# Attention and a Fourier-mixing block on one Trainium2 core: token fold with repeated operands, whole 128x128 transposes, and a new order of the work

## The chip, the cores and the metric

The kernel runs on one core of a Trainium2 chip. The engines of the core work side by side: PE multiplies matrices, DVE, ACT and POOL work on vectors, and SP here only issues DMA transfers, as ACT and POOL also do. Every engine runs its own list of instructions strictly in order and waits at an instruction whose inputs are not there. The metric is the time of one execution in microseconds (us); the number that counts is the median of several runs.

## The reference, cut to what matters

```python
def reference(q, k, v, w1, w2):            # q, k, v: 4 batches, 8 heads, 768 tokens, 64
    s = q @ k.T / 8 - slope[h] * dist      # keys kept: the first 8, and the last 96 before the query
    x = softmax(where(keep, s, -1e9)) @ v  # -> x: 4 x 768 x 512
    u = x + real(fft(fft(x, axis=tokens), axis=features))
    un = (u - mean(u)) / sqrt(var(u) + 1e-6)
    return u + relu(un @ w1) @ w2          # w1: 512 x 2048, w2: 2048 x 512
```

## The kernel before, in words

**Three layers of work.** PE's work falls into units, and every unit carries a name. `A0` to `A76` are attention units: scores of a band of keys (`sc`, L729, L737, L743), or `pav`, the product with v (L822). `M0` to `M32` are mixing units, which do the two Fourier transforms as matrix products: `pf` (L1013) folds the tokens of batch 0 and `px` (L1165) spreads them, `py` (L1105) is the product along one axis, `pu` (L1192) the one along the other; its result with x added is `u`. The transposes of the normalised `un` into `unT` are M units too (`ptu`, L1309). `H0` to `H95` are blocks of the first product of the feed-forward part (`ph`, L1339: 8 matmuls of 128 x 256), and `G0` to `G66` are parts of the second.

**Pair-chunks.** Each batch's tokens are cut into 3 pair-chunks of 256 tokens, 12 in all, numbered c=0 to 11, each with 8 `ph` blocks. Chunks 0 and 1 do the second product plainly (`pg`, L1370, 64 matmuls of 128 x 512 together). From chunk 2 on it is done with seven products in place of eight (`pgA` and `pgD`, L1484, evacuated by DVE at L1502). These need four sums per chunk of halves of the hidden layer, `s1` to `s4`, each one 128 x 1024 addition in 16 bits (`eg`, `sb`, `hT`). `s2`, `s3` and `s4` wait for earlier sums of their chunk, and `s1` for the chunk's hidden blocks.

**Transposing un.** For c=0 to 2 PE does it, with 64 x 64 transposes into one PSUM tile `ptu`, copied out at L1321. For c=3 to 11 the DMA does it from SP's queue (L1292).

**Fold.** The token fold (two units on PE, each for two heads' columns) forms six sums of x's token blocks, with the identity, minus the identity and plus or minus half of it as weights: 32 matmuls of 128 columns into one `pf` tile.

**x by way of DRAM.** For batch 1 and later, x is written to DRAM when it is finished (`xd`: L872 and L874, from ACT's queue) and read back twice in the order in which `u` needs it: `xr` in rows by SP's queue (L884), and mirrored rows by an indirect DMA of POOL (L887), which needs the small table `back`. DVE adds them when it evacuates `pu` (L1232 and L1244). `distk` is another table, from which ACT and DVE make the masks `mk` of batches 2 and 3.

**w1 and w2** come as eight DMAs of 512 KB from POOL's queue (L1674). Part j of w1 holds hidden blocks 2j and 2j+1.

**What sets the order.** A class `Plan` holds a table `ORDER`, one list of names for each engine: unit names for PE, and for the others names such as `H5.0` (an evacuation or a follow-up of unit H5) and `T.91` (a DMA, a table, a sum). `Plan.run` issues the work in that order; its costs and due times place instructions that are not free in the list, but on each engine the list decides. Evacuations can be on ACT (`hT`, L1344) or DVE (L1345), as the list says. Where a list names `T.91`, the xr read-back of batch 1, as next on SP, everything behind it in SP's list stands until its inputs are there.

Of the kernel before, what the change touches and what calls it, by code (L numbers as in the profile page):

```python
# [24 lines left out]
class Plan:  # L25
# [9 lines left out]
    MIX = 1.3  # L35
    LANDED = {"HW": 0.55, "SW": 1.3}
    LAT = {"ACT": 0.14, "DVE": 0.12, "POOL": 0.08}
# [84 lines left out]
    def op_go(self, eng, name, start):  # L122
# [6 lines left out]
        if eng == "POOL":  # L129
            self.ports.append((start, end, 1 if dma else 0 if outs and outs[0][0] in ("vB", "kB") else 2))  # L130
        if dma:
            at = max(max(end + 0.55, 5.5) if eng == "POOL" else end + lat + 2.7 * (lat == 1.0 and end > 3.5), self.now)
# [19 lines left out]

    SHARED = {"kB": 1, "vB": 1, "sid": 1, "f1": 0, "f2": 0, "f3": 0, "z": 0, "g0": 0, "w": 0, "s": 0, "w2a": 0, "w2t": 0, "ex": 0}
# [3 lines left out]
    def beside(self, start, cost, kind):  # L157
# [4 lines left out]
        if names:  # L162
            s = self.op_start("POOL", names[-1])
            if s is not None:
                p = self.made[names[-1]]
                ports = ports + [(max(s, start), max(s, start) + p[0]["POOL"][0], 1 if p[7] else 0 if p[3] and p[3][0][0] in ("vB", "kB") else 2)]
# [15 lines left out]
    def move(self, go=False):  # L182
# [38 lines left out]
    def unit_start(self, unit):  # L221
# [7 lines left out]
        if not there:  # L229
# [114 lines left out]
def act(n):  # L344
    return 0.1 + n / 1180.0
# [10 lines left out]
def pool(n):  # L356
    return 0.16 + n / 1080.0


@with_exitstack  # L360
def kernel(
# [156 lines left out]
    def load_v(b, hp):  # L518
        h0 = 2 * hp
        if b >= FB:  # L520
# [3 lines left out]
            swq(whole, 1.08, [("avdone", b - 2), ("wl", 7)], [("v", b, hp, t) for t in range(2)], (1536, 0.93), False)  # L524
            return
        if b == 1:
            for t in range(2 - hp % 2 * 2):
# [3 lines left out]
                swq(four, 1.08, [], [("v", b, hp, t), ("v", b, hp + 1, t)], (1536, 0.93))  # L531
            return
        for t in range(2):
# [3 lines left out]
            swq(run, 0.85, ([("avdone", b - 2), ("wl", 7)] if b > 1 else []), [("v", b, hp, t)], (768, 0.93), b < 2)  # L537
# [4 lines left out]
    def load_qk(b, hp):  # L542
# [3 lines left out]
        for w, src in enumerate((q, k)):  # L546
            if b >= FB:
                for h in range(2):
# [4 lines left out]
                    swq(run, 0.85, free(tag, ti) + [("wl", 7)], [("qk", n, w, h)], (768, 0.93), False)  # L553
# [25 lines left out]
            if n == 4:  # L579
# [5 lines left out]
                swq(two, 1.08, free(tag, ti), [("qk", n, w), ("qk", n + 1, w)], (1536, 1.53))  # L585
# [7 lines left out]
            swq(run, 0.85, free(tag, ti), [("qk", n, w)], (768, 1.53))  # L593
# [110 lines left out]
    def score(b, hp, g):  # L704
# [3 lines left out]
        def run(start, ring):  # L708
# [37 lines left out]
            e = pl.pe((0.45, 0.45, 0.34)[g] if pem else 0.24, start, "64x64" if pem else "64x32")  # L746
# [203 lines left out]
    def fold_0():  # L950
# [53 lines left out]
        def fold_pe(hp):  # L1004
            cols = slice(hp * P, (hp + 1) * P)

            def run(start, ring):
                zy()
                pf = bank(ring, f"pf_{hp}")
                for n, terms in enumerate(ZS):  # L1010
                    o = pf[:, n // 4, (n % 4) * P:(n % 4 + 1) * P]
                    for x, (w, i) in enumerate(terms):
                        nc.tensor.matmul(o, w, X[0][:, i, cols], start=(x == 0), stop=(x == len(terms) - 1))  # L1013
# [775 lines left out]
```

## Time and profile before

| | |
|---|---|
| runs | 247.54, 247.75, 249.1 us; median 247.75 us |
| profiled execution | 245.87 us, with a span of 244.1 us; granted TensorE clock 0.991 |
| PE busy | 232.0 us (95% of the span) |
| DVE busy | 193.4 us (79%) |
| ACT busy | 138.8 us (57%) |
| POOL busy | 114.8 us (47%) |
| DMA moved | 32.85 MB |

The span is from the first to the last instruction of the profiled execution; 1.8 us of its own time lie outside the span. The median of the other runs is 1.9 us above the profiled one. Busy PE counts a matmul from its start to a modelled end, and matmuls overlap their neighbours, so starts are more exact than busy times: a unit's cost is read from the start of its first matmul to the start of the next unit.

### The profile page before, as it was taken

What the parts mean: (1) busy time and instruction counts of PE and PEld (TensorE: products, weight loads), DVE (VectorE), ACT (ScalarE), POOL (GpSimd) and SP (SyncE); (2) the same over time, 40 slices, a digit from 0 to 9 for tenths busy, and PEclk for the clock granted to TensorE, in tenths of its full rate; (3) what the DMA queues carried; (4) which work ended last, traced back from release to release, by engine and by line L of the source; (5) the groups of instructions that cost most, each with busy time, mean ns of one, the idle gap of its engine ahead of it and who ended that gap; (6) DMA issues with size and microseconds to landing.
All of it is one profiled execution on the core that took longest, in us unless ns stands there. A gap on an engine that the chain in (4) does not pass through costs nothing.

```text
span 244.1 us, 7606 instructions
## 1 busy us (share of the span) xinstructions
PE 232.0 (95%) x3251; PEld 191.2 (78%) x3251; DVE 193.4 (79%) x420; ACT 138.8 (57%) x226; POOL 114.8 (47%) x164
## 2 busy tenths in 40 slices
PE   7679899999999999999999999999999999999993
PEld 2557776878677667788989888898889898888883
DVE  2559997879972789999999889889998755846483
ACT  2368788864657468658357788364534651434200
POOL 8998898866590038999059056500300320011020
PEclk9997999999999999999999999999999999999999
DMA  6999999999999999999999979220570330040212
GB/s 170 181 169 145 157 235 172 197 190 196 110 145 152 234 179 205 117 135 110 242 184 285 135 84 156 46 33 13 174 258 4 77 99 0 1 130 1 89 72 99
DMA packets 95938, 32.85 MB, mean 135 GB/s; under 512 B 84160, under 2 KB 92480, under 8 KB 95904
## 3 DMA queue, kind: packets, MB, share of 16 engines
q0 software_dynamic: 66176, 17.06, 71.7%
q1 hardware_dynamic: 26560, 12.56, 25.1%
q10 hardware_dynamic: 3168, 2.75, 4.1%
q8 instruction: 25, 0.41, 0.7%
q14 instruction: 9, 0.07, 0.1%
HBM read 31.44 MB, written 8.65 MB: 164 GB/s over the span
## 4 chain that ended last, share of the span: by engine, by line
PE 67%; DMA 14%; DVE 5%; ACT 5%; POOL 3%; issue 3%; SPq 1%; POOLq 0%
PE ph L1339 29%; PE pgD L1484 14%; PE pgA L1484 10%; DMA qk<-in_q_dram 4%; DMA v<-in_v_dram 4%; PE py L1105 3%; DMA hT<-in_q_dram 3%; PE pg L1370 3%; PE pav L822 3%; ACT ex L766 2%; DMA back<-backm 2%; DMA xr<-xd,back 2%; PE sc L737 2%; PE pu L1192 1%; ACT mk L1657 1%
## 5 line engine op out<-in xcount | busy, mean ns | idle before, releaser
L1339 PE MATMUL ph<-unT,w 128*128 128x256 f16 x768 | 94.4, 273 | 0.8 <-issue 0.4
L1339 PEld LDWEIGHTS <-w 128*128 128x128 f16 x768 | 73.6, 98 | 12.5 <-issue 1.2
L1344 ACT ACTIVATE hT<-ph 128x512 f16<-128x512 f32 x73 | 42.9, 596 | 54.6 <-PE ph L1339 52.6
L1484 PEld LDWEIGHTS <-hT 128*128 128x128 f16 x320 | 31.0, 98 | 4.3 <-issue 0.4
L1285 POOL TENSOR_SCALAR sm<-sm 128x2 f32<-128x2 f32 x12 | 3.4, 284 | 58.2 <-ACT un L1278 57.8
L763 ACT ACTIVATE er<-sc 128x1024 f16<-128x1024 f32 (+1 forms) x24 | 22.3, 951 | 11.4 <-PE sc L737 8.2
L1345 DVE TENSOR_SCALAR hT<-ph 128x512 f16<-128x512 f32 x23 | 15.7, 687 | 12.7 <-PE ph L1339 12.7
L766 ACT ACTIVATE ex<-sc 128x1024 f16<-128x1024 f32 (+1 forms) x24 | 21.7, 955 | 7.1 <-PE sc L743 6.9
L1502 DVE SCALAR_TENSOR_TENSOR u<-pgA,sm,u 128x256 f32<-128x256 f32 (+1 forms) x30 | 16.9, 568 | 6.4 <-PE pgA L1484 6.0
L1502 DVE SCALAR_TENSOR_TENSOR u<-pgD,sm,u 128x512 f32<-128x512 f32 (+1 forms) x21 | 15.2, 722 | 3.5 <-PE pgD L1484 3.3
L1355 POOL DMA_INDIRECT out_dram<-u,back x4 | 4.5, 1120 | 27.5 <-DVE rev L1140 16.3
L887 POOL DMA_INDIRECT xr<-xd,back x3 | 4.8, 1602 | 25.4 <-PE pg L1370 16.1
L1370 PE MATMUL pg<-w,hT 128*128 128x512 f16 x64 | 16.0, 379 | 0.0
L1118 ACT ACTIVATE zy<-py 128x1024 f16<-128x1024 f32 (+1 forms) x13 | 11.1, 857 | 8.4 <-PE py L1105 6.1
L778 DVE TENSOR_TENSOR ex<-er,mk 128x1024 f16<-128x1024 f16 (+1 forms) x24 | 15.1, 646 | 0.7 <-ACT er L763 0.7
L1278 ACT ACTIVATE un<-un 128x512 f16<-128x512 f16 x24 | 15.0, 625 | 1.1 <-DMA unT<-un 1.1
L552 POOL DMA_DIRECT2D qk<-in_k_dram x16 | 13.7, 903 | 1.2 <-DMA w<-in_moe_w_ch_dram 0.8
L1269 ACT ACTIVATE un<-u,sm 128x512 f16<-128x512 f32 x19 | 13.1, 717 | 1.9 <-DVE sm L1251 0.7
L552 POOL DMA_DIRECT2D qk<-in_q_dram x16 | 13.6, 870 | 0.0
L822 PEld LDWEIGHTS <-ex 128*128 128x128 f16 x352 | 12.4, 97 | 1.1 <-ACT ex L766 0.4
L834 DVE TENSOR_TENSOR x<-pav,rc 128x384 f16<-128x384 f32 x24 | 12.6, 554 | 0.6
L822 PE MATMUL pav<-v,ex 128*128 128x65 f16 x224 | 12.9, 193 | 0.2
(170 smaller groups left out, 492.9 us busy)
## 6 DMA issues: line engine op xcount, KB each, us to landing
w<-in_moe_w_ch_dram POOLq DMA_DIRECT2D x8, 512.0 KB, 13.4
out_dram<-u SPq DMA_DIRECT2D x15, 256.0 KB, 3.0
v<-in_v_dram POOLq DMA_DIRECT2D x12, 192.0 KB, 5.8
qk<-in_k_dram POOLq DMA_DIRECT2D x16, 96.0 KB, 5.4
qk<-in_q_dram POOLq DMA_DIRECT2D x16, 96.0 KB, 4.5
xr<-xd SPq DMA_DIRECT2D x3, 512.0 KB, 4.6
xd<-x ACTq DMA_DIRECT2D x2, 768.0 KB, 4.5
v<-in_v_dram POOLq DMA_DIRECT2D x8, 96.0 KB, 7.0
```

The source lines that it names most:

```text
L552: nc.gpsimd.dma_start(qk16[n][:, w, :, h], src[b, h0 + h].rearrange("(i m) d -> m i d", m=P))
L763: A(mine(), cut(pa), AF.Exp, 0.0, 0.125)
L766: A(cut(expst[hp][:, :, g * 512:g * 512 + (384 if g == 2 else 512)]), cut(pa), AF.Exp, 0.0, 0.125)
L778: VT(o, mine(), m, op=ALU.mult)
L822: nc.tensor.matmul(o[:, s * 65:(s + 1) * 65], lhsT, w, start=(a == 0), stop=(a == len(ops) - 1), skip_group_check=True)
L1278: A(x, x, AF.Square, accum_out=MV[c][:, a, 2:3])
L1339: nc.tensor.matmul(ph[:, a * CH:(a + 1) * CH].rearrange("p (x m) -> p x m", x=2), W1[0][:, d, jb * P:(jb + 1) * P], UNT[c][:, :, d, :], st ...
L1344: pl.later([("ACT", act(512), lambda: A(dst, ph, AF.Relu)), ("DVE", dve(512), lambda: V.tensor_scalar_max(dst, ph, 0.0))], [], e, [("h", c ...
L1345: ("DVE", dve(512), lambda: V.tensor_scalar_max(dst, ph, 0.0))],
L1370: nc.tensor.matmul(pg, HT[c][:, jb, t * P:(t + 1) * P], W2[0][:, jb, :], start=(jb == 0), stop=(jb == NJ - 1))
L1484: nc.tensor.matmul(o, lhs(j), rhs(j), start=(first and j == 0), stop=(j == NK - 1), skip_group_check=True)
L1502: V.scalar_tensor_tensor(o, x, r(t), acc, op0=ALU.mult, op1=ALU.add)
```

## The change

**Costs of the plan.** Some 30 constants of `Plan` get other values (for instance the time of an indirect read 1.1 to 1.6, the fixed part of an ACT instruction 0.1 to 0.055, a 64-row transpose unit 0.27 to a 128-row one 0.46). No instruction follows from them by itself; the list `ORDER` decides.

**Fold.** The same 32 x 128 columns are computed in 21 matmuls: one weight block is applied to a block of x that is broadcast to 2 or 4 outputs.

**Transposes** for c=0 to 2: 8 of 128 x 128 in place of 32 of 64 x 64, into one bank, copied out contiguously.

**Sums** `s1` to `s4` may run on POOL from chunk 3 on. The new list puts 18 of them there: all four of chunks 6 and 7, three each of chunks 3 and 4, and one each of chunks 8, 9, 10 and 11. Of the copies `vB` (a pair for each head pair's v) POOL gives three pairs to DVE and takes one, and the three `rev` copies of batch 1 (mirrored rows) go to DVE.

**Order.** PE's list is the same up to the unit M11 (the first `ptu`) and new from there; the lists of the other engines are the same up to about the same time. The unit M6's copy moves from DVE to ACT. On ACT the `xd` writes of batch 1 (T.89, T.90) now stand right behind the last write to that x.

```diff
-        ZS = (((one, 0), (one, 3), (one, 1), (one, 4), (one, 2), (one, 5)), ...
+        ZT = ((one, 0, 0, 4, 1), (one, 3, 0, 2, 2), (neg, 3, 1, 2, 2), (one, 4, 0, 2, 1), ...
...
-                for n, terms in enumerate(ZS):
-                    o = pf[:, n // 4, (n % 4) * P:(n % 4 + 1) * P]
-                    for x, (w, i) in enumerate(terms):
-                        nc.tensor.matmul(o, w, X[0][:, i, cols], start=(x == 0), stop=(x == len(terms) - 1))
+                for x, (w, i, n, k, step) in enumerate(ZT):
+                    o = pf[:, n // 4].rearrange("p (n m) -> p n m", m=P)[:, n % 4:n % 4 + (k - 1) * step + 1:step]
+                    nc.tensor.matmul(o, w, X[0][:, i, cols].unsqueeze(1).to_broadcast([P, k, P]), start=..., stop=..., ...)
...
-                    for i in range(2):
-                        for h in range(2):
-                            r, o, x = slice(64 * i, 64 * i + 64), d * P + 64 * h, 64 * (a * ND + d)
-                            nc.tensor.transpose(pt[64 * h:64 * h + 64, i, x:x + 64], un[r, a, o:o + 64], idn[r, r], ...)
+                    nc.tensor.transpose(pt[:, 0, (a * ND + d) * P:(a * ND + d + 1) * P], un[:, a, d * P:(d + 1) * P], idn)
...
-        def s1():
-            VT(new(0), block(1, 0), block(1, 1), op=ALU.add)
+        def s1(on=V):
+            on.tensor_tensor(new(0), block(1, 0), block(1, 1), op=ALU.add)
...
+        def slow(fn):
+            return [("POOL", pool2(NK * P), lambda: fn(nc.gpsimd))] if c > 2 else []
...
-        pl.later([("DVE", us, s1)], hs + sfree(0), 0.0, [("s", c, 1)], rank=1)
+        pl.later([("DVE", us, s1)] + slow(s1), hs + sfree(0), 0.0, [("s", c, 1)], rank=1)
... ORDER, from the unit M11 on: on PE
-  M11 M13 A44 H2 H7 A43 H4 H3 M12 A42 H0 H1 A41 H12 G4 H13 H11 G0 H6 H5 M14 G1 G5 ...
+  M11 H5 H7 M12 A44 H2 M13 H6 H3 A43 H0 H4 A41 H10 H1 A42 H11 H9 G4 G0 M14 G5 H8 G1 ...
... and on SP
-  T.6 T.0 T.9 T.136 T.35 T.127 T.133 T.128 G7.1 T.134 T.91 G3.1 T.10 T.137 ...
+  T.6 T.0 T.9 T.91 T.35 T.10 T.127 G7.1 G3.1 T.133 T.128 T.136 T.134 T.137 ...
```

The three places at which the new list matters most for what follows are shown as lists of instructions. The first is PE right after the first transpose unit `ptu` of chunk 0 (names: `un_1193` and `un_1170` are chunk 0's un, `w_0_881` a part of w1, and weight loads stand between the matmuls). Before:

```order
L1309 MATMUL ptu_1252<-ident,un_1193 64x64
...
L1192 MATMUL pu_1287<-t_75,zy_1038 128x128
...
L822 MATMUL pav_3_1307<-v_85,ex_83 128x65
...
L1339 MATMUL ph_2_1340<-unT_1304,w_0_904 128x256
...
L1339 MATMUL ph_7_1354<-unT_1304,w_0_904 128x256
```

With the change:

```order
L1316 MATMUL ptu_1228<-ident,un_1170 128x128
...
L1345 MATMUL ph_5_1250<-unT_1240,w_0_881 128x256
...
L1345 MATMUL ph_7_1263<-unT_1240,w_0_881 128x256
...
L1316 MATMUL ptu_1274<-ident,un_1259 128x128
...
L832 MATMUL pav_3_1284<-v_85,ex_83 128x65
```

The two units that stood between the first transposes and the first hidden block, `pu` and `pav`, now come later; two hidden blocks follow at once, of w1's parts 2 and 3, and then chunk 1's transposes.

The second place is SP's list behind its first table loads (`out` are stores, `qkT` are transposes of batches 2 and 3). Before:

```order
L1608 DMA misc_73<-distm 128x1280
L631 DMA_TRANSPOSE qkT_11_1658<-qk_5_1124 128x6x128
L1608 DMA distk_74<-distkm 128x640
L631 DMA_TRANSPOSE qkT_8_1768<-qk_2_1488 128x6x128
L631 DMA_TRANSPOSE qkT_10_1802<-qk_4_1504 128x6x128
L631 DMA_TRANSPOSE qkT_8_1768<-qk_2_1488 128x6x128
L1386 DMA out_0_dram<-u_2_948 128x512
L631 DMA_TRANSPOSE qkT_10_1802<-qk_4_1504 128x6x128
L884 DMA xr_1_1853<-xd_1_1780 128x2048
L1386 DMA out_0_dram<-u_2_948 128x512
L1608 DMA back_79<-backm 128x4
```

With the change:

```order
L1617 DMA misc_73<-distm 128x1280
L894 DMA xr_1_1603<-xd_1_1530 128x2048
L1617 DMA distk_74<-distkm 128x640
L1617 DMA back_79<-backm 128x4
L641 DMA_TRANSPOSE qkT_8_1693<-qk_2_1355 128x6x128
L1392 DMA out_0_dram<-u_2_909 128x512 x2
L641 DMA_TRANSPOSE qkT_10_1729<-qk_4_1409 128x6x128
L641 DMA_TRANSPOSE qkT_8_1693<-qk_2_1355 128x6x128
```

The read-back `xr` went from behind five transposes to the head of SP's list, and the tables `distk` and `back` stand right behind it.

The third place is POOL around the sums of chunks 6 and 7 (`hT_3020` and `hT_3421` are their hidden layers; the rows of 128x2 are a normalisation's square root, the `xr` row is the indirect read of batch 3). Before:

```order
L793 COPY vB_88<-v_85 128x528
L795 COPY vB_88<-v_85 32x528
L1285 TENSOR_SCALAR sm_2997<-sm_2997 128x2
L1286 TENSOR_TENSOR sm_2997<-sm_2997,mhalf 128x2
L887 DMA xr_3761<-xd_3691,back 128x1024
L1355 DMA out_dram<-u_2996,back 1536x1024
```

With the change:

```order
L805 COPY vB_87<-v_85 32x528
L1454 TENSOR_TENSOR eg<-hT_3020 128x1024
L1460 TENSOR_TENSOR sb<-eg,hT_3020 128x1024
L1295 TENSOR_SCALAR sm_2909<-sm_2909 128x2
L1296 TENSOR_TENSOR sm_2909<-sm_2909,mhalf 128x2
L1457 TENSOR_TENSOR hT_3020<-hT_3020 128x8x128
L1465 TENSOR_TENSOR sb<-hT_3020,sb 128x1024
L1454 TENSOR_TENSOR eg<-hT_3421 128x1024
L1460 TENSOR_TENSOR sb<-eg,hT_3421 128x1024
L897 DMA xr_3682<-xd_3583,back 128x1024
L1457 TENSOR_TENSOR hT_3421<-hT_3421 128x8x128
L1465 TENSOR_TENSOR sb<-hT_3421,sb 128x1024
```

Eight 128 x 1024 additions, which DVE did before, now stand here one behind the other, with the root of a normalisation and the indirect read of batch 3 between them.

More of the change, by code (lines that the diff above doesn't have):

```diff
@@ L35 @@
     MIX = 1.3
+    ALONE = 1.54
     LANDED = {"HW": 0.55, "SW": 1.3}
-    LAT = {"ACT": 0.14, "DVE": 0.12, "POOL": 0.08}
+    LAT = {"ACT": 0.18, "DVE": 0.12, "POOL": 0.08}
     def __init__(self):
@@ L129, in op_go @@
         if eng == "POOL":
-            self.ports.append((start, end, 1 if dma else 0 if outs and outs[0][0] in ("vB", "kB") else 2))
+            self.ports.append((start, end, 1 if dma else 0 if outs and outs[0][0] in ("vB", "kB", "ts", "w1s", "s") else 2))
         if dma:
-            at = max(max(end + 0.55, 5.5) if eng == "POOL" else end + lat + 2.7 * (lat == 1.0 and end > 3.5), self.now)
+            at = max(max(end + 0.95, 5.33) if eng == "POOL" else end + lat + 2.7 * (lat == 1.0 and end > 3.5), self.now)
             cell = [self.NEVER]
@@ L165, in beside @@
                 p = self.made[names[-1]]
-                ports = ports + [(max(s, start), max(s, start) + p[0]["POOL"][0], 1 if p[7] else 0 if p[3] and p[3][0][0] in ("vB", "kB") else 2)]
+                ports = ports + [(max(s, start), max(s, start) + p[0]["POOL"][0], 1 if p[7] else 0 if p[3] and p[3][0][0] in ("vB", "kB", "ts", "w1s", "s") else 2)]
         for a, b, dma in ports:
@@ L186, in move @@
         sw = any(k == "SW" for k, h in act)
-        both = [h[2] for k, h in act if k != "AQ" or sw]
+        nxt = self.q["SW"][1][0] if len(self.q["SW"]) > 1 else self.NEVER
+        us = {k: h[2] * (self.ALONE if k == "SW" and h[2] < 2.0 and nxt > self.now + 1e-9 else 1.0) for k, h in act}
+        both = [us[k] for k, h in act if k != "AQ" or sw]
         each = sum(both) * (self.MIX if len(both) > 1 else 1.0) / 1000.0
@@ L190, in move @@
         t = min([self.now + h[1] * rate[k] for k, h in act] + [h[0] for k, h in heads if h[0] > self.now + 1e-9] + [self.NEVER])
+        if sw and nxt > self.now + 1e-9:
+            t = min(t, nxt)
         if not go:
@@ L344, in act @@
 def act(n):
-    return 0.1 + n / 1180.0
+    return 0.055 + n / 1180.0
 def dve(n):
@@ L357, in pool, with pool2 @@
     return 0.16 + n / 1080.0
+def pool2(n):
+    return 0.2 + n / 450.0
 @with_exitstack
@@ L523, in whole @@
                                     v[b, h0:h0 + 2].rearrange("h (i m) d -> m (h i) d", m=P))
-            swq(whole, 1.08, [("avdone", b - 2), ("wl", 7)], [("v", b, hp, t) for t in range(2)], (1536, 0.93), False)
+            swq(whole, 1.08, [("avdone", b - 2), ("wl", 7)], [("v", b, hp, t) for t in range(2)], (1536, 0.97), False)
             return
@@ L530, in four @@
                                         v[b, h0:h0 + 4].rearrange("h (i m t) d -> t m (h i) d", m=64, t=2)[t])
-                swq(four, 1.08, [], [("v", b, hp, t), ("v", b, hp + 1, t)], (1536, 0.93))
+                swq(four, 1.08, [], [("v", b, hp, t), ("v", b, hp + 1, t)], (1536, 0.97))
             return
@@ L584, in two @@
                                         src[b, h0:h0 + 4].rearrange("h s d -> (h s) d").rearrange("(m p t) d -> p m (t d)", p=P, t=2))
-                swq(two, 1.08, free(tag, ti), [("qk", n, w), ("qk", n + 1, w)], (1536, 1.53))
+                swq(two, 1.08, free(tag, ti), [("qk", n, w), ("qk", n + 1, w)], (1536, 1.42))
                 continue
@@ L852, in part @@
             m = k.stop - k.start
-            pl.later([("DVE", 0.17 + 0.03 * m + m * dve(384), lambda: norm(po, k))], free(*XT[b]), e,
+            pl.later([("DVE", 0.08 + 0.03 * m + m * dve(384), lambda: norm(po, k))], free(*XT[b]), e,
                      [("x", b, hp, z) for z in range(k.start, k.stop)], CD(b, ring), ring=ring, rank=RA(b))
@@ L890, in bounce @@
         pl.later([("SP", 0.38, rd)], xw + free("xr", b), 0.0, [("xr", b)], lat=2.0, dma=(128, 10.4))
-        pl.later([("POOL", 1.1, rg)], xw + [("xr", b), ("c", "back")], 0.0, [("xg", b)], dma=(128, 4.94), rank=0)
+        pl.later([("POOL", 1.6, rg)], xw + [("xr", b), ("c", "back")], 0.0, [("xg", b)], dma=(128, 4.94), rank=0)
     def fold_s(b):
@@ L940, in fold_s @@
             pl.later([("DVE", 2 * dve2(2 * cw) + 0.6 * (b + n == 0), f2)], [("f1", b, n)] + free("ww", IW(b, n)), 0.0, [("f2", b, n)])
-            pl.later([("DVE", (4 if b else 2) * dve2(cw), f3)], [("f2", b, n)], 0.0, [("f3", b, n)])
+            pl.later([("DVE", (3.45 if b else 2) * dve2(cw), f3)], [("f2", b, n)], 0.0, [("f3", b, n)])
             if b == 0:
@@ L1142, in r0 @@
             Y[(b, 0, 3, "r")], Y[(b, 3, 3, "r")] = rev[:, 0], rev[:, 1]
-        pl.later([("POOL", 0.8, lambda: r0(nc.gpsimd.tensor_copy)), ("DVE", 0.3, lambda: r0(V.tensor_copy))], [("y", b, 0, 3), ("y", b, 3, 3)] + free("rev0", b), 0.0,
+        pl.later([("POOL", 1.1, lambda: r0(nc.gpsimd.tensor_copy)), ("DVE", 0.3, lambda: r0(V.tensor_copy))], [("y", b, 0, 3), ("y", b, 3, 3)] + free("rev0", b), 0.0,
                  [("y", b, 0, 3, "r"), ("y", b, 3, 3, "r")], [("free", "zy", 2 * b + 1)])
@@ L1272, in centre @@
         for a in range(2):
-            pl.later([("ACT", 0.62, lambda a=a: un("ACT", a)), ("DVE", 1.3 if c < 2 else 0.38, lambda a=a: un("DVE", a))],
+            pl.later([("ACT", 0.62, lambda a=a: un("ACT", a)), ("DVE", 1.3 if c < 2 else 0.55, lambda a=a: un("DVE", a))],
                      [("u", c, a)] + free("un", c), 0.0, [("un", c, a)])
@@ L1286, in rstd @@
             nc.gpsimd.tensor_tensor(r, r, mhalf, op=ALU.pow)
-        pl.later([("POOL", 0.82, rstd)], [("ss", c, 0), ("ss", c, 1)], 0.0, [("rstd", c)], rank=2)
+        pl.later([("POOL", 1.25, rstd)], [("ss", c, 0), ("ss", c, 1)], 0.0, [("rstd", c)], rank=2)
     def nt_dma(c):
@@ L1357, in st @@
                                          in_=UT[c].rearrange("p r d -> p (r d)"), in_offset=None)
-        pl.later([("POOL", 1.1, st)], needs, 0.0, [], [("free", "u", c + pl.U0)] * 2, dma=(128, 11.25), rank=0)
+        pl.later([("POOL", 1.25, st)], needs, 0.0, [], [("free", "u", c + pl.U0)] * 2, dma=(128, 11.25), rank=0)
     def pg_unit(c, t, part):
@@ L1610, in dma_const @@
             ways = ways + [("POOL", 0.66, lambda: nc.gpsimd.dma_start(dst, src.ap()))]
-        pl.later(ways if soon else ways[:1], needs, 0.0, [tok], lat=1.0 if soon else 3.2, dma=us)
+        pl.later(ways if soon or tok == ("dk",) else ways[:1], needs, 0.0, [tok], lat=1.0 if soon else 3.2, dma=us)
     with tc.manual_schedule():
@@ L1684 @@
                     load_qk(1, hp)
[L1685 removed]
+            swq(lambda i=i: wload(i), 0.77, [], [("w1", i)], (512, 5.24))
         for hp in range(HP):
```

60 lines of the change are left out of this document (30 added, 30 removed), and 58 rows, old and new, of the table ORDER.

## The prediction

> **What bounds the kernel now.** I read the page's engine row first, then busy times by stretch, then the chain of waits for the price of each unit on PE, and last PE's timeline for what is lost between units.
>
> ```profile
> PE 232.0 (95%) x3251; PEld 191.2 (78%) x3251; DVE 193.4 (79%) x420; ACT 138.8 (57%) x226; POOL 114.8 (47%) x164
> 70.00:87.00 17.00, 17.00 (x180) 11.74 (x177) 9.12 (x15) 10.42 (x19) 2.80 (x4) 1.00 1.43 196
> 87.00:112.00 25.00, 24.05 (x406) 19.61 (x390) 24.00 (x56) 18.25 (x30) 21.79 (x27) 1.00 1.50 143
> 112.00:163.00 51.00, 51.00 (x768) 44.63 (x752) 47.19 (x101) 34.59 (x56) 23.80 (x31) 1.00 1.00 144
> 163.00:231.00 68.00, 68.00 (x657) 61.20 (x655) 49.91 (x103) 29.83 (x57) 7.26 (x12) 1.00 0.27 79
> ```
>
> PE sets the end: 95% of the span, and in the windows' rows, where PE, PEld, DVE, ACT and POOL follow one another, it is all but full from 70 us on at a granted clock of 1.00 (the number after POOL's count; then the DMA's share and GB/s). A reordering can only win the gaps that PE still has. DVE is half idle at 70 to 87 us and full (24.00 of 25.00) at 87 to 112. POOL has room late, 7.26 busy of 68 us.
>
> How much is in the gaps? The prices of units, start to start, are in the chain of waits:
>
> ```profile
> 56.95 0.67 PE pav L822 x22
> 63.71 0.38 PE ptu L1309 x32
> 70.47 0.87 PE ph L1339 x8
> 71.34 0.86 PE pg L1370 x4
> 109.90 1.75 PE pgD L1484 x16
> 134.18 0.89 PE pu L1192 x16
> ```
>
> From the first `ptu` at 47.02 us to 104.90 us, where the new order differs most, PE ran these (matmuls by line and form):
>
> ```profile
> L1339 PE MATMUL ph<-unT,w 128*128 128x256 f16 x232 | 29.0, 273 | 0.8 <-issue 0.4 <-DMA unT<-un 0.4
> L1370 PE MATMUL pg<-w,hT 128*128 128x512 f16 x64 | 16.0, 379 | 0.0
> L737 PE MATMUL sc<-qkT 64*32 64x256 f16 x102 | 3.4, 275 | 0.0
> L737 PE MATMUL sc<-qkT 64*32 64x128 f16 x84 | 3.2, 217 | 0.2 <-ACT er L763 0.2
> 96.18 0.63 PE L737 MATMUL sc<-qkT 64*32 64x256 f16 x38
> 96.74 1.92 PE L1339 MATMUL ph<-unT,w 128*128 128x256 f16 x16
> ```
>
> The last two rows, of the timeline, price the scores: 38 in 0.56 us. So: 232 `ph` matmuls are 29 units of 0.87 = 25.2; 64 `pg` are 16 of 0.86 = 13.8; 186 scores and 6 of another line 2.8; and 4 `pav`, 3 `pu`, 3 `py`, 3 `ptu` and 4 halves of `pgA` and `pgD` (`py` and these have the shape of the `pgD` row, 0.87 for 8) are 2.7, 2.7, 2.6, 1.1 and 3.5. That makes 54.4 of 57.9 us: **3.5 us are lost.** Where, the same timeline shows:
>
> ```profile
> 53.50 0.39 PE L1339 MATMUL ph<-unT,w 128*128 128x256 f16 x2 [0.38 <-issue]
> 93.15 0.60 PE L1105 MATMUL py<-t,eA 128*128 128x256 f16 x4
> 94.34 1.91 PE L1339 MATMUL ph<-unT,w 128*128 128x256 f16 x16 [0.37 <-DMA unT<-un]
> 104.90 1.03 PE L1484 MATMUL pgA<-misc,hT 128*128 128x256 f16 x8 [0.31 <-DVE u L1502]
> ```
>
> Counted by starts these gaps are a little larger than in the brackets: the `py` unit at 93.15 has 6 matmuls, a share of 0.65 in 0.87, and the next unit starts 1.19 later, 0.54 lost. With 0.65 at 53.5, 0.31 and 0.18 around 100, 0.47 at 104.9 and 0.16 behind the second `ptu`, **2.3 us are waits with a cause.** The other 1.2 are some 14 steps of 0.09 at which PE goes to or from the scores' 64x32 tiles. From 105 us on I find 1 us more of such steps, and no wait at all between 164 and 231 us.
>
> **The change part by part.** *Fold: 0.* It runs before the new order:
>
> ```profile
> 27.58 0.56 PE L1013 MATMUL pf<-x,ident 128*128 128x128 f16 x7
> 29.47 0.86 PE L652 MATMUL pt<-ident,qk 128*64 128x128 f16 x24
> 35.11 0.41 PE L729 MATMUL sc<-misc 64*64 64x512 f16 x4 [0.32 <-DVE zy L1020]
> ```
>
> One fold takes 29.47 - 27.58 = 1.89 us for 32 matmuls, 0.056 to 0.059 for 128 columns. The columns stay the same, so 21 matmuls take 32 x 0.056 = 1.8; the two folds save 0.1 each at most. The third row's wait for DVE takes that up, as DVE's chain isn't shortened. Should broadcast operands be read slower, no row prices them; at twice the columns' time the folds cost 2 x 1.8 = 3.6, which I take as a bound that nothing here supports. *Transposes: 0.* Eight of 128 columns are 8 x 0.056 = 0.45 against 0.38 for a `ptu` now; three units, +0.2 at most.
>
> *Blocks of c=0 as w1 lands: +1.0 at the start, -0.8 of waits removed.* The last part of w1:
>
> ```profile
> L1674 POOL DMA_DIRECT2D w<-in_moe_w_ch_dram x1: 803/803/803, 37.4 to 37.4; - x1
> DMA to landing us min/median/max: 15.8/15.8/15.8
> 46.88 1.22 DVE L1176 COPY u<-px 128x1024 f32<-128x1024 f32 x1
> 48.02 0.68 DVE L1321 COPY unT<-ptu 128x1024 f16<-128x1024 f16 x1
> ```
>
> It lands at 37.4 + 15.8 = 53.2 us, and the `ph` at 53.50 waits for it; in the new order the blocks of that part come behind four others, so 0.65 and the 0.16 after it go. But the first block now stands right behind the first `ptu`, which ends at 47.4, with nothing between, and needs `unT`. DVE gives it at 48.6 now, behind a copy of 1.22 that ACT takes over in the new order; so about 0.3 earlier, at 48.3 to 48.4: PE waits 1.0. Before, `pu` and `pav` (0.93 and 0.67) covered this.
>
> *x of batch 1 by DRAM first: the wait for it goes; new ones of 1.0 come.*
>
> ```profile
> 65.70 0.57 SPq L1608 DMA_DIRECT2D distk<-distkm  x1
> 82.21 0.52 SPq L884 DMA_DIRECT2D xr<-xd  x1
> L874 ACTq DMA_DIRECT2D xd<-tt x2: 582/618/655, 73.1 to 75.7; - x2
> DMA to landing us min/median/max: 6.3/6.7/7.2
> 92.95 0.87 DVE L1244 SCALAR_TENSOR_TENSOR u<-pu,xr 128x384 f32<-128x384 f32 x1 [0.41 <-DMA xr<-xd,back]
> L887 POOL DMA_INDIRECT xr<-xd,back x3 | 4.8, 1602 | 25.4 <-PE pg L1370 16.1
> ```
>
> Now the writes leave at 73.1 to 75.7 us and the read-back at 82.2, behind the transposes; DVE stands for the mirrored rows at 92.95, just where it is full. In the new order the writes leave when x is ready, which my walk with the prices above puts at 62; they land 6.7 later, near 70 with two of them, and the read-back, at the head of SP's list, lands near 75 and the mirrored one near 80. `u` of chunks 3 and 4 so comes 5 to 8 us earlier, and its work goes into DVE's half-idle stretch. That takes away the 0.54 (`unT` of chunk 3 late) and lightens what lies behind 0.31, 0.18 and 0.47, all of them DVE's or ACT's backlog. The price: SP stands at the read-back, and `distk`, issued at 65.7 before, goes out at 70.5. ACT and DVE make masks from it; `py` copies queue behind these on ACT. By my walk the `pu` unit M17 then waits 0.6 for them and the first `pgD` 0.4 for w2's sums on DVE.
>
> So in this stretch the waits with a cause go from 2.3 to 1.0 + 0.6 + 0.4 = 2.0: **-0.3**. The scores are cut into 13 groups, not 15, and two groups are four steps of 0.09: **-0.4**.
>
> *Sums on POOL: 0 for the forecast, and the widest unknown.* 18 of the 40 sums leave DVE. No row shows POOL adding tiles of this size; the nearest rows:
>
> ```profile
> L1451 DVE TENSOR_TENSOR hT<-hT 128x1024 f16<-128x1024 f16 x10 | 7.5, 750 | 0.0
> L1141 POOL COPY rev<-zy x3: 390/405/877, 44.6 to 149.1; 128x256 f16<-128x256 f16 x3
> L795 POOL COPY vB<-v x15: 617/617/1137, 21.7 to 155.7; 16x528 f16<-16x528 f16 x8, 32x528 f16<-32x528 f16 x7
> 131.25 1.14 POOL L795 COPY vB<-v 32x528 f16<-32x528 f16 x1
> 131.23 0.68 DVE L1448 TENSOR_TENSOR eg<-hT 128x1024 f16<-128x1024 f16 x1
> ```
>
> Copies of 256 and 528 columns differ by 0.23 us, 0.83 ns a column, so 1024 are 1.03. At the copy's price per input, two inputs make 2.0; the lower bound is 1.0, one stream. The last two rows show a clash: beside one DVE addition of 16 bits POOL's copy took 1.14 for 0.62, so each such neighbour adds 0.5. I take one, **2.5 us**; two are 3.1, three 3.5 (the upper bound). The Trainium skill, GPSIMD Engine Reference, section 3.1 on elementwise work side by side, counts some 2.6 cycles per element for such an addition at 1.2 GHz and advises DVE; by it 1024 columns are 2.2 us, an estimate from that page, and it speaks against the move. Its Advanced Engine Details and Errata, VectorE Performance Modes, says that the two engines block each other on a shared port, which the row of 1.14 bears out.
>
> What may a sum cost? The tightest place is chunk 7. From the end of its last hidden block to the product that needs `s4`, PE's new list has 12 units of 8 matmuls (0.87; four `pg`-like ones among them), one of 16 (1.75), one `pu` (0.89) and a `py` of 2 (0.22): 13.3 us. POOL needs for that four sums, 1.6 of the indirect read between them, 0.6 for the block's evacuation and 0.15 of handing over: 4p + 2.35 fits to p = 2.7. Chunk 6 has 14.8 us for 4p + 1.9, up to 3.2, and the others more. At 2.5 nothing waits, narrowly. DVE gets 18 x 0.75 = 13.5 us back, off the path.
>
> **Sum:** -0.3 - 0.4 = -0.7 us on the span of 244.1 gives 243.4, and the profiled execution's own 245.87 becomes 245.2. The median of the runs lies 1.9 above that execution, so 247.75 - 0.7 = **247.0 us**. About 1% (2.5 us) is what a measurement can tell from no change.
>
> **The rivals.** *A. The waits with a cause vanish nearly all*, because the read-back in time empties DVE's peak and my 1.0 at the first block and 1.0 behind the masks are overlapped by work I placed too late: -2.3 - 0.4 = -2.7, 245.0 us. For it: every cause but w1 traces to DVE or a DMA that moves earlier. Against: the first `ptu` has nothing behind it but `ph` of the same chunk. Its bound is all 3.5 lost now, 244.3. Chance 0.25. *B. POOL's sums come late*: at 3.5 us each, from 2.7 on, chunk 7's fourth sum holds PE by 4 x (3.5 - 2.7) = 3.0 and chunk 6's by 1.1, so +4.1 - 0.7 = 251.1 us, slower. For it: the row of 1.14, and in the stretch from 112 to 163 DVE is busy 47.19 of 51 us, so a neighbour is nearly always there; against: many of its instructions are not of 16 bits. Chance 0.28. *C. The read-back holds up SP more than it gives*: `distk` 5 us late makes ACT stand 1.4 us at its first mask, and `py` and score evacuations behind it hold PE: +1.4 - 0.7 = 248.4. Chance 0.09. The forecast itself has 0.38.
>
> **How the numbers follow.** Faster by over 1%: A, 0.25. Slower by over 1%: B, 0.28. Within: the forecast and C, 0.47. The likeliest's own range is 245.8 to 248.4, with its terms doubled or gone. The whole range goes to A's bound and B's time: 244.3 to 251.2.
>
> **What would show it.** Right: `ph` behind the first `ptu` with about 1 us of wait for `unT`; no wait at w1's last part; `xr` of batch 1 landed by 76 us and its mirrored rows by 81; DVE's `u` of chunk 4 before 88 us; POOL's additions of 128x1024 near 2.5 us and no wait of `pgA` or `pgD` for POOL. Wrong: additions above 2.7 us with PE waiting in chunk 7 (B), masks that ACT waits for (C), waits of 47 to 105 us under 1 us (A), or `pf` above 2 us.

## The result, and the profile after

The changed kernel takes **260.52 us** (median of four runs, 259.92 to 261.19) against 248.43 us (247.54 to 249.69) for the kernel before on the same chip: a ratio of 1.0484, 95% interval 1.0424 to 1.0543. Ratios and intervals, here and below, leave out runs more than 1.5% above the fastest of the same kernel; medians and ranges keep them. Forecast were 247.0 us and a range up to 251.2. The profiled span is 258.0 us, 13.9 longer. The page of the changed kernel, its engines and PE's slices:

```profile
PE 234.4 (91%) x3157; PEld 191.8 (74%) x3157; DVE 207.9 (81%) x413; ACT 134.3 (52%) x222; POOL 151.4 (59%) x175
PE   7877898899999999958967999999967999999994
```

PE, which had no gap late, now has two: in the 18th to 22nd slice and in the 30th and 31st. DVE was to be relieved of 13.5 us and is 14.5 us busier (207.9 against 193.4). Busy times by stretch of the changed kernel (PE, PEld, DVE, ACT, POOL, then PE's clock), and behind them the middle stretch of the kernel before:

```profile
47.95:105.17 57.22, 57.22 (x683) 44.91 (x684) 46.16 (x103) 36.42 (x64) 32.33 (x41) 1.00 1.41 168
105.00:163.00 58.00, 50.50 (x707) 42.15 (x705) 51.40 (x91) 30.72 (x52) 36.14 (x34) 0.94 1.07 135
163.00:245.00 82.00, 78.01 (x842) 68.71 (x841) 69.06 (x121) 32.99 (x64) 36.74 (x29) 1.00 0.27 71
```

```profile
105.00:163.00 58.00, 58.00 (x878) 50.90 (x878) 54.09 (x117) 38.51 (x64) 30.67 (x40) 1.00 1.08 142
```

Up to 105 us nothing is lost: the unit that began at 104.90 us before begins at 105.17, and 2.5 us more of PE's work are done by then. By starts, taking every unit's usual price off as in the prediction, PE loses 1.8 us between the first `ptu` and that unit, where it lost 3.5 before. After it PE loses 18.2 us, where it lost 1.5. What the early part of the change was to do is in these rows of the changed kernel (`xd` writes and their landing; the read-back on SP; the two `u` on DVE; the first hidden block on PE):

```profile
L884 ACTq DMA_DIRECT2D xd<-tt x2: 632/642/653, 61.3 to 62.0; - x2
DMA to landing us min/median/max: 6.5/6.8/7.2
69.27 0.34 SPq L894 DMA_DIRECT2D xr<-xd  x1
81.15 0.69 DVE L1242 SCALAR_TENSOR_TENSOR u<-pu,xr 128x512 f32<-128x512 f32 x1 [1.69 <-PE pu L1202]
83.78 0.84 DVE L1254 SCALAR_TENSOR_TENSOR u<-pu,xr 128x384 f32<-128x384 f32 x1
47.95 1.91 PE L1345 MATMUL ph<-unT,w 128*128 128x256 f16 x16 [0.87 <-DVE sm L1231]
```

The two `u` begin 6.0 and 9.2 us earlier than before and wait for no DMA. Now the same kernel's timelines around its costliest wait, POOL first, then DVE, then PE:

```profile
128.71 2.13 POOL L1454 TENSOR_TENSOR eg<-hT 128x1024 f16<-128x1024 f16 x1 [0.32 <-ACT hT L1350]
130.92 2.18 POOL L1457 TENSOR_TENSOR hT<-hT 128x1024 f16<-128x1024 f16 x1
129.00 2.12 DVE L936 TENSOR_TENSOR zy<-eA,ww 128x512 f16<-128x512 f16 x1
131.04 2.33 DVE L937 TENSOR_TENSOR zy<-eA,ww 128x512 f16<-128x512 f16 x1
131.51 1.91 PE L1345 MATMUL ph<-unT,w 128*128 128x256 f16 x16
136.94 1.89 PE L1115 MATMUL py<-t,ww 128*128 128x256 f16 x8 [3.51 <-DVE ww L1073]
138.62 3.62 PE L1345 MATMUL ph<-unT,w 128*128 128x256 f16 x16
```

Two DVE operations of 512 columns take 2.12 and 2.33 us, where they took 0.41 and 0.42 before; each ends 0.28 us behind the end of a POOL sum. Their results feed the chain of DVE operations for which PE stands 3.51 us. The wait at 113 us has the longest such operation behind it (DVE, POOL, PE):

```profile
110.36 4.95 DVE L788 TENSOR_TENSOR ex<-er,mk 128x1024 f16<-128x1024 f16 x2
111.53 2.22 POOL L1460 TENSOR_TENSOR sb<-eg,hT 128x1024 f16<-128x1024 f16 x1
116.03 0.37 PE L832 MATMUL pav<-v,ex 128*128 128x65 f16 x7 [2.90 <-ACT er L773]
```

The first of the two `ex` alone takes 4.48 us, for a usual 0.68. It began 1.17 us before the sum, while POOL issued DMAs, and ended 1.1 us after it, so it stood for longer than the sum lasted. POOL's sums themselves are not slow: the 18 last 2.1 to 2.8 us. Which DVE operations are stretched, the groups by form tell, first of the changed kernel and then of the kernel before:

```profile
L788 DVE TENSOR_TENSOR ex<-er,mk 128x1024 f16<-128x1024 f16 x16 | 16.0, 1005 | 1.3 <-ACT er L773 1.2
L1071 DVE TENSOR_TENSOR eA<-zy 128x1536 f16<-128x1536 f16 x3 | 4.7, 1581 | 0.0
L1511 DVE SCALAR_TENSOR_TENSOR u<-pgD,sm,u 128x512 f32<-128x512 f32 x19 | 14.1, 743 | 1.2 <-PE pgD L1493 1.0
```

```profile
L778 DVE TENSOR_TENSOR ex<-er,mk 128x1024 f16<-128x1024 f16 x16 | 10.7, 683 | 0.4 <-ACT er L763 0.4
L1061 DVE TENSOR_TENSOR eA<-zy 128x1536 f16<-128x1536 f16 x3 | 2.9, 957 | 0.1
L1502 DVE SCALAR_TENSOR_TENSOR u<-pgD,sm,u 128x512 f32<-128x512 f32 x19 | 14.2, 747 | 2.9 <-PE pgD L1484 2.7
```

Additions and products of two 16-bit tiles rise from a mean of 683 to 1005 ns and from 957 to 1581; the evacuation of PSUM in the third row of each keeps its 0.74 us. All 32 DVE operations that read PSUM beside a sum in this profile keep their usual time.

### The profile page after: what moved, and what is told of

Read it like the earlier page. It is cut to its first block, busy times and chain, and to the rows that moved or that the text cites. A ratio compares the mean times of both kernels' runs of the same rounds, so it can differ in the third digit from the quotient of the medians.

```text
span 258.0 us, 7427 instructions
## 1 busy us (share of the span) xinstructions
PE 234.4 (91%) x3157; PEld 191.8 (74%) x3157; DVE 207.9 (81%) x413; ACT 134.3 (52%) x222; POOL 151.4 (59%) x175
## 4 chain that ended last, share of the span: by engine, by line
PE 61%; DVE 24%; DMA 6%; issue 4%; POOL 3%; ACT 2%; DVEq 0%; POOLq 0%
PE ph L1345 24%; PE pgD L1493 8%; PE pgA L1493 7%; PE pg L1376 5%; PE py L1115 4%; DVE u L1511 3%; DVE ex L788 3%; DMA hT<-in_q_dram 3%; DMA tt<-in_k_dram 3%; DVE x L844 3%; PE pu L1202 2%; PE pav L832 2%; PE sc L747 2%; DVE eA L1071 1%; PE pt L662 1%
## 5 line engine op out<-in xcount | busy, mean ns | idle before, releaser
L1345 PE MATMUL ph<-unT,w 128*128 128x256 f16 x768 | 96.7, 276 | 0.9 <-DVE sm L1231 0.9
L1350 ACT ACTIVATE hT<-ph 128x512 f16<-128x512 f32 x69 | 40.7, 597 | 67.7 <-PE ph L1345 66.0
L1351 DVE TENSOR_SCALAR hT<-ph 128x512 f16<-128x512 f32 x27 | 18.3, 685 | 12.8 <-PE ph L1345 12.6
L788 DVE TENSOR_TENSOR ex<-er,mk 128x1024 f16<-128x1024 f16 (+1 forms) x24 | 20.2, 853 | 2.4 <-ACT er L773 2.2
L1465 POOL TENSOR_TENSOR sb<-hT,sb 128x1024 f16<-128x1024 f16 x4 | 9.2, 2298 | 17.0 <-PE pgA L1493 17.0
L1115 PE MATMUL py<-t,ww 128*128 128x256 f16 x80 | 12.5, 290 | 7.2 <-DVE ww L1073 5.9
L1457 POOL TENSOR_TENSOR hT<-hT 128x1024 f16<-128x1024 f16 x6 | 12.9, 2155 | 8.3 <-DVE mk L1454 8.2
L1279 ACT ACTIVATE un<-u,sm 128x512 f16<-128x512 f32 x20 | 14.2, 719 | 6.1 <-DVE sm L1246 5.0
L1376 PE MATMUL pg<-w,hT 128*128 128x512 f16 x64 | 15.5, 379 | 0.0
L1115 PEld LDWEIGHTS <-ww 128*128 128x128 f16 x80 | 7.7, 103 | 10.3 <-DVE ww L1073 6.4
L1295 POOL TENSOR_SCALAR sm<-sm 128x2 f32<-128x2 f32 x12 | 5.2, 437 | 16.9 <-ACT un L1288 16.5
```

The lines of the kernel that those rows point to most:

```text
L788: VT(o, mine(), m, op=ALU.mult)
L1115: nc.tensor.matmul(o, lhsT, rhs, start=(x == 0), stop=(x == len(ops) - 1))
L1345: nc.tensor.matmul(ph[:, a * CH:(a + 1) * CH].rearrange("p (x m) -> p x m", x=2), W1[0][:, d, jb * P:(jb + 1) * P], UNT[c][:, :, d, :], st ...
L1350: pl.later([("ACT", act(512), lambda: A(dst, ph, AF.Relu)), ("DVE", dve(512), lambda: V.tensor_scalar_max(dst, ph, 0.0))], [], e, [("h", c ...
L1351: ("DVE", dve(512), lambda: V.tensor_scalar_max(dst, ph, 0.0))],
L1376: nc.tensor.matmul(pg, HT[c][:, jb, t * P:(t + 1) * P], W2[0][:, jb, :], start=(jb == 0), stop=(jb == NJ - 1))
```

## The experiments

Three theories. **P**: a POOL sum keeps DVE's operations on 16-bit tiles waiting for its whole length. **L**: the sums are only late. **O**: the new order itself makes the waits after 105 us. The recorded expectations call what DVE and POOL would have to share "the port".

**1. All 18 sums back on DVE** (in ORDER alone, at the times at which POOL began them):

```diff
-  POOL: ... T.152 ... T.208 ... T.210 T.209 ... T.255 T.251
+  DVE: ... G20.0 A54.1 T.208 A53.1 T.125 T.210 T.124 ... (18 names)
```

> The changed kernel with its 18 sums back on DVE, in DVE's list where POOL began them in the profile of the changed kernel. Theory P (a sum on POOL keeps DVE's 16-bit operations waiting for its whole length): no DVE addition of 16 bits above 1.2 us, no wait of PE over 1.5 us after 105 us, 245.5 to 249 us. Rival O (the new order itself, with x read back first, makes the waits after 105 us): 256 us or more. Rival L (the sums are merely late, because one takes POOL 2.2 us): 245.5 to 249 us as well; the other runs tell it from P.

Measured: 252.51 us (250.27 to 254.80), ratio 1.0241 (1.0155 to 1.0327) to before. The additions are back at 686 ns, the waits of 3.1, 2.5 and 1.5 us (by starts; 2.90, 2.38 and 1.29 in the brackets) are gone, and 8 of the 12 lost us return; O's 256 is out. The time is above my range all the same: one wait of 1.8 us is left at 131 us, behind a table that SP issues late, and several of 0.3 to 0.6 where I had put a sum ahead of something more urgent.

**2. The kernel before with the same sums on POOL:**

```diff
-        pl.later([("DVE", us, s1)], ...
+        pl.later([("DVE", us, s1)] + slow(s1), ...      (and 18 names from DVE's list to POOL's)
```

> The kernel before with the same 18 sums on POOL, in POOL's list at the times at which DVE began them. P and L: 255 us or more, with DVE additions of 2 us beside POOL's. O: 247 to 250 us.

Measured: 261.52 us (four runs: 256.26, 261.08, 261.96 and 262.63; before 247.75). The sums alone, in the old order, cost 8.5 to 14.9 us, where the whole change costs 12; the runs lie too far apart for a ratio. In its profile, which is of the slowest run, PE loses some 15.5 us after the unit that began at 104.9 us before, of them 5.2 within one `py` unit.

**3 and 4. Added work that nobody reads.** The kernel before, all sums on DVE, and 18 POOL operations on a spare tile at the times of the 18 sums:

```diff
+    SPARE = kon.tile([P, 1024], FP16, ...)
+    nc.gpsimd.tensor_tensor(SPARE, flat[:, 0:1024], flat[:, 512:1536], op=ALU.add)     # run 3
+    nc.gpsimd.tensor_copy(SPARE, flat[:, 0:1024])                                       # run 4
```

> The kernel before, every sum left on DVE, with 18 added POOL additions of 128x1024 in 16 bits on a spare tile that nobody reads, at the times of the 18 sums. P: DVE operations of 2 us beside them, 252 to 262 us though nobody waits for the added work. L: no more than 1 us, 247 to 249 us, since no result is late. O: 247 to 249 us.

> The same with 18 POOL copies of 128x1024 (one input) in place of the additions. P as I hold it (an operation with two inputs keeps the port, a copy yields to DVE, as the copy of 1.14 us beside a DVE addition of 0.68 showed): 247.5 to 249 us, POOL's copies stretched, DVE's additions not. If any POOL work holds DVE up: 250 to 255 us, about half of the additions' price, as a copy is about half as long.

Measured: 269.03 us (ratio 1.0887, 1.0823 to 1.0951) with additions, 251.89 us (1.0203, 1.0132 to 1.0275) with copies. This parts P from L: no result is late, and still 18 additions cost 21.3 us, 1.2 us each; that is above the 262 us that I had allowed. That POOL's own later work is late does not show as a cause either: in this profile no DVE or ACT operation waits for POOL, and PE waits 0.7 us for it, as before. The 1.2 us is not the price of a sum in the changed kernel: here DVE still does its own 18 sums, which can be held too, and part of it is PE's clock, granted at 0.968 on the mean against 0.991. Of the kernel with additions, and then of the one with copies, the added tile's line and DVE's groups by form:

```profile
L1754 POOL TENSOR_TENSOR spare<-t x18: 2109/2224/2722, 114.1 to 258.8; 128x1024 f16<-128x1024 f16 x18
L777 DVE TENSOR_TENSOR ex<-er,mk 128x1024 f16<-128x1024 f16 x16 | 17.3, 1098 | 0.4 <-ACT er L762 0.4
L833 DVE TENSOR_TENSOR x<-pav,rc 128x384 f16<-128x384 f32 x24 | 12.6, 554 | 0.6
```

```profile
L1754 POOL COPY spare<-t x18: 1027/1048/1406, 116.0 to 242.5; 128x1024 f16<-128x1024 f16 x18
L777 DVE TENSOR_TENSOR ex<-er,mk 128x1024 f16<-128x1024 f16 x16 | 13.0, 824 | 0.4 <-ACT er L762 0.4
```

My own expectation fell, and its alternative, 250 to 255 us, came: copies do not yield. In the timelines of the kernel with copies, at 182 us, POOL runs four copies in a row (one row here) while DVE's operations stand between them:

```profile
181.97 5.12 POOL L1754 COPY spare<-t 128x1024 f16<-128x1024 f16 x4
182.01 1.43 DVE L1062 TENSOR_TENSOR ww<-eA 128x768 f16<-128x768 f16 x1
183.37 1.38 DVE L1063 TENSOR_TENSOR ww<-eA 128x768 f16<-128x768 f16 x1
184.67 0.74 DVE L1501 SCALAR_TENSOR_TENSOR u<-pgD,sm,u 128x512 f32<-128x512 f32 x1
```

0.56 us of DVE work takes 1.43 and 1.38: it waits some 0.9 us for a copy to end, and the next copy, at 1.26 us for a usual 1.03, waits for it. The evacuation of PSUM behind them takes its 0.74. A copy costs 0.2 us of the end, where an addition costs 1.2; it holds DVE for about half as long or less, and that DVE's slack takes up short waits first is my reading, not shown.

**5. Each POOL sum in four pieces:**

```diff
-            on.tensor_tensor(new(0), block(1, 0), block(1, 1), op=ALU.add)
+            for r in four slices of 256 columns: on.tensor_tensor(o[:, r], x[:, r], y[:, r], op=op)
```

> The changed kernel with each POOL sum cut into four additions of 256 columns, nothing else moved. If the port is held for one instruction at a time (P): a DVE operation beside it waits for one piece, some 0.6 us, and goes between two pieces; the longest DVE additions fall from 2.3 to about 1.3 us, the sums take POOL 2.4 to 3.5 us each, and the time lies between the changed kernel (260.5) and the one with its sums on DVE (252.5): 253 to 258 us. If the two engines only share a bandwidth: no change, 259 to 262 us.

Measured: 253.70 us (ratio 1.0281, 1.0207 to 1.0355). Same place, same sums, same engine: POOL, then DVE, of this kernel:

```profile
126.53 2.91 POOL L1456 TENSOR_TENSOR eg<-hT 128x256 f16<-128x256 f16 x4
127.17 0.94 DVE L936 TENSOR_TENSOR zy<-eA,ww 128x512 f16<-128x512 f16 x1
128.03 0.89 DVE L937 TENSOR_TENSOR zy<-eA,ww 128x512 f16<-128x512 f16 x1
```

DVE now gets in between two pieces: 0.9 us for what took 2.1 and 2.3. The two `ex` that took 4.95 us in the changed kernel take 1.73 here, with the same DMA issues and the same sum in pieces beside them. So the hold goes with the length of one instruction, and 6.8 us of the loss go with it, at no less work on POOL (2.91 us for a sum of 2.13). That is as far as run 1 got, within the noise; against the kernel before 2.8% are still lost.

**6. The eight sums of chunks 6 and 7 alone back on DVE:**

```diff
-  POOL: ... T.224 T.225 M23.11 T.227 T.226 T.230 T.231 T.190 T.233 T.232 ...
+  DVE: the same eight names
```

> The changed kernel with the eight sums of chunks 6 and 7 alone back on DVE, ten left on POOL. P: the waits of PE before 165 us stay (the 3.1 at 112 us and the 3.7 at 132 us with the slower clock behind it), those of 2.5 and 1.5 us at 188 to 194 us go: 255 to 258 us.

Measured: 259.19 us (257.68 to 261.73; ratio 1.0469, 1.0400 to 1.0539), above what I expected. The wait of 2.5 us at 188 is gone, but the chain of short DVE waits there stays, as in run 1. The other ten, six of them of chunks 3 and 4, make nearly the whole loss; the two costliest waits, at 113 and 133 us, lie beside sums of chunks 3 and 4. The profile is of the slowest of the four runs, and its clock was at half for 10.2 us after 119 us, against 6.8 in the changed kernel, which may hide part of the gain.

**7. A version with the sums on DVE and seven names moved:**

```diff
-  PE: M11 H5 H7 M12 A44 ...           SP: T.102 T.212 T.206 T.34 ...
+  PE: M11 A44 H5 H7 M12 ...           SP: T.102 T.34 T.212 T.206 ...
   DVE: T.216 after T.147, T.226 after G38.0, T.195 before T.230, G21.0 before A59.0, A50.1 before A60.0
```

> The kernel with the sums back on DVE and seven names moved: on PE the unit A44 (pav) ahead of the first two hidden blocks, on SP the table T.34 ahead of two stores, on DVE five operations to where their inputs are there. If what that kernel lost against the one before is only where I put the sums, and the 1.0 us in front of the first hidden block: 246 to 248.5 us, level with before. If the new order has a loss of its own: 250 us or more.

Measured: 247.70 us (12 runs, 246.38 to 249.19), ratio 1.0004 (0.9970 to 1.0038). With the sums on DVE and these seven names moved, the change is level with the kernel before: O, in this form, has no loss of its own, and no gain either.

**8. That version with the read-back put back behind four transposes on SP:**

```diff
-  SP: T.9 T.91 T.35 T.10 T.127 G7.1 G3.1 T.133 T.128 T.136 T.134 ...
+  SP: T.9 T.35 T.10 T.127 G7.1 G3.1 T.133 T.128 T.136 T.91 T.134 ...
```

> The kernel with seven names moved, its read-back of batch 1 put back behind four transposes and two stores on SP, nothing else. By my prediction's step the early read-back takes 0.5 us of waiting off PE and lightens another 1.0: so 248 to 249.5 us, up to 1.5 slower than with it. If it is worth nothing: 247 to 248 us.

Measured: 249.90 us, ratio 1.0101 (1.0064 to 1.0139): 2.2 us slower than run 7, a little above my range. The tables `distk` and `back` go out ahead of the read-back here, so it is not the read-back's place alone that differs. Its timelines show the read-back on SP 9.0 us later than in run 7 (69.98 there), `u` 1.9 us later on DVE (81.71 there; the read-back lands at 83.5, though the bracket names `ph`), and then PE waiting 1.3 us for an ACT operation; how that wait hangs on `u`, and where the rest of the 2.2 us goes, was not traced:

```profile
78.97 0.52 SPq L893 DMA_DIRECT2D xr<-xd  x1
83.64 0.69 DVE L1241 SCALAR_TENSOR_TENSOR u<-pu,xr 128x512 f32<-128x512 f32 x1 [4.32 <-PE ph L1344]
88.67 0.41 PE L746 MATMUL sc<-qkT 64*32 64x256 f16 x18 [1.30 <-ACT er L772]
```

**9 to 12. Fold and transposes apart** (the hunks of the diff, each alone on the kernel before, both on it, and both taken out of run 7):

> The kernel before with the fold of 21 matmuls and the whole 128x128 transposes alone, its order untouched. My sum: 0, within 0.5 us of before (the fold -0.1 each and absorbed, three transpose units +0.07 each). If broadcast operands are read at half speed: the fold 3.6 us each, up to 2 us slower.

> The kernel before with the fold of 21 matmuls alone. If the 1% comes from the fold: 249.5 to 251 us; if not, 247.5 to 249 us. In both the fold's units last 1.86 us.

> The kernel before with the 128x128 transposes alone: units of 0.45 us against 0.38. If the 1% comes from the transposes: 249.5 to 251 us; if not, 247.5 to 249 us.

> The kernel with seven names moved, with the old fold of 32 matmuls and the old 64x64 transposes. If fold and transposes cost 1% of themselves (as the kernel before with both alone suggests): 245 to 246.5 us, faster than before. If that 1% was only the old order's thin cover for its late transfers: 247 to 248.5, as with the new ones.

| | median us | ratio to before (95%) |
|---|---|---|
| fold alone | 247.58 | 0.9990 (0.9954 to 1.0026) |
| transposes alone | 248.81 | 1.0051 (1.0016 to 1.0085) |
| both, old order | 250.37 | 1.0100 (1.0054 to 1.0147) |
| run 7 with the old ones | 250.01 | 1.0085 (1.0047 to 1.0122) |

The units are as priced: a fold lasts 1.86 us (1.89 before), a `ptu` 0.45 (0.38). The fold alone costs nothing, the transposes alone 0.5%, both in the old order 1%; but in the new order it is the old ones that cost 0.8%. So neither has a fixed price, and two expectations were missed: 0 for both in the old order, and at most 248.5 us for run 7 with the old ones. In the profile of both in the old order, PE waits longer for a part of w1, and DVE for x's read-back, which neither hunk touches:

```profile
49.65 1.92 PE L1335 MATMUL ph<-unT,w 128*128 128x256 f16 x16 [1.00 <-DMA w<-in_moe_w_ch_dram]
88.20 0.69 DVE L1232 SCALAR_TENSOR_TENSOR u<-pu,xr 128x512 f32<-128x512 f32 x1 [1.99 <-DMA xr<-xd]
```

PE's other new waits there, 0.6 to 0.9 us each, are for ACT and DVE. Each list of names was laid out with its own durations, and small shifts may meet the transfers and the other engines differently. That explanation is only argued: which shift does it was not tried.

## Why the prediction was wrong, point by point

**The step that failed is the sentence "DVE gets 18 x 0.75 = 13.5 us back, off the path", with the 0 for POOL's sums.** The sums were free for POOL, as worked out (2.1 to 2.8 us each, 2.5 forecast; at the tight place in chunk 7 no product waited for POOL), but not for DVE, whose busy time rose by 14.5. The relief was too large as well: the change also gives DVE copies that POOL did, and in run 1, with every sum on DVE, DVE is busy 197.3 us, 3.9 more than before. The changed kernel spares DVE those 18 sums, some 12 us, and is still 10.6 us busier than run 1: by these numbers, an estimate, DVE stood some 23 us. Every sign that I had named for being right was there, from the 1.0 us before the first block to no wait for POOL's sums, and none of them concerned DVE's operations.

The row that decided was in the prediction: POOL's copy took 1.14 us beside a DVE addition. I read it one way only, as the copy being stretched by DVE, and priced the clash on POOL's side, where there was slack, and not on DVE's, which was busy 47 of 51 us. Turned round, the same row prices it: if the one that comes second waits until the other is done, a DVE operation beside a sum of 2.2 us takes up to 2.2 longer. The Trainium skill says so on its page SBUF — State Buffer, section "SBUF: two separate sides": the pair of ports that DVE and GpSimd share is a lock held for the whole instruction by the one that starts first. Runs 3 to 5 agree that the hold goes by instructions, and the operations with which DVE reads PSUM (0.74 and 0.55 us throughout) were not held. The `ex` of 4.48 us does not fit so simply: by the profile it started before the sum and stood 3.8 us. Why is open; without POOL sums no DVE operation beside POOL's DMA issues was stretched by more than 0.7 us.

**Rival B** was on the right side with the wrong mechanism and the wrong size: it let the sums come late from 2.7 us on, 251.1 us in all (its 3.0 us is 4 x 3.5 + 2.35 - 13.3; the product as written gives 3.2). They were not late at 2.2, and the loss was 12. The range ended at B's time, so a cost that none of the cases held lay outside it.

**The stretch up to 105 us** came out better than forecast, -1.7 us against -0.7. The wait of 1.0 before the first hidden block was there (1.03 by starts, 0.87 in the row's bracket); the wait for w1's last part was gone; the writes left at 61.3 to 62.0 (62 forecast), the read-back went out at 69.3 and the two `u` came 6.0 and 9.2 us earlier (5 to 8 forecast). The waits of 0.6 and 0.4 behind the masks, priced by my walk, were not there, which is rival A's "work I placed too late", and rival C's held-up masks did not come. Run 8 gives the early read-back 2.2 us, more than the 0.5 to 1.5 of my steps; why more was not traced.

**The fold** at 0 was right. **The transposes** were right as a unit and wrong as a sum: 0.2 us at most forecast, 1.2 us measured alone in the old order. **The order as a whole**, with seven names moved, was worth 0 us (run 7), not -0.7: what the stretch up to 105 us gains is given back after it. By starts PE loses some 1.6 us in that stretch of run 7 and 4.7 after it, against 3.5 and 1.5 before.

## What to carry to other kernels

Before work goes to POOL to relieve DVE, price it on both engines: not only whether POOL is in time, but which DVE operations run beside it and how long they would stand. A stretched operation in a trace prices the clash for the other engine too. Count also what DVE takes over in exchange. If such work must be on POOL, cut it into short instructions (253.7 against 260.5 us here; left on DVE, with the order tuned, 247.7), or put it where DVE reads PSUM, which no run here tried. And name a sign for the engine that is to be relieved, not only for the one that gets the work.

## What the runs showed of the hardware that I had not expected

- **The hold goes both ways and copies take part in it.** A POOL addition of 128x1024 in 16 bits lasts 2.1 to 2.8 us and holds a DVE operation on 16-bit tiles mostly by 1 to 2 us, by 3.8 at most in the changed kernel; a copy of the same size lasts 1.03 to 1.41 and holds it by 0.9 in the rows above, by 1.4 at most. Four pieces of 256 columns take 2.9 us in place of 2.1 but hold it some 0.5 in the rows above. It is not the 16 bits: in run 3 an operation on 128x2 in 32 bits took 1.50 us for a usual 0.17. The operations that read PSUM all kept their time.
- **A long wait of PE costs more than its length.** PE waited 3.5 us, from 133.4 to 136.9 us, in the changed kernel, and the granted clock was half from 135.6 to 142.4 us, so for 5 us of PE's work behind the wait:

```profile
136.90:142.00 5.10, 5.06 (x24) 3.51 (x25) 3.81 (x9) 1.62 (x2) 0.56 (x1) 0.50 1.03 123
```

Sixteen `ph` matmuls took 3.62 us there (the row at 138.62), not 1.91: 0.8 us for each of three units, 2.5 us in all. A wait of 2.9 us at 113 us left the clock at 1.00 in that profile, but in run 6 the same wait was followed by a slower clock, so its length alone does not decide. In all fourteen traces the changes of the clock lie on a grid of 3.41 us. The stretches of that grid in which these waits lie, two of the changed kernel and then one of run 6 (PE's busy time is the second number):

```profile
111.69:115.10 3.41, 1.44 (x14) 1.14 (x12) 3.41 (x2) 0.15 (x1) 3.41 (x3) 1.00 2.04 139
132.16:135.57 3.41, 1.26 (x12) 0.88 (x9) 3.38 (x6) 2.15 (x4) 3.10 (x3) 1.00 0.97 254
```

```profile
116.04:119.45 3.41, 1.02 (x10) 0.77 (x8) 3.41 (x3) 0.56 (x1) 3.41 (x4) 1.00 1.79 130
```

Behind the first the clock stayed, behind the other two it was half: the same wait cost more where more of it fell into one stretch. Where the line lies is open, and PE's busy time alone does not draw it: in the kernel before, the clock fell at 17.8 us behind a stretch in which PE was busy 1.8 us of 3.41. The Trainium skill, TensorE: Matmul & The Clock Gate, section "What's actually happening", gives a window of about 3.4 us that runs freely, which agrees with the grid; but it has the clock fall after an idle window, and none of these was idle throughout.
